# Four tiles ahead of the first projection: the odd 64 columns transposed twice by TensorE instead of normalised twice

## The chip, the cores and the metric

The kernel runs on one core of one Trainium2 chip. The metric is the time of one execution in device microseconds (us). Three runs of the kernel before took 221.12, 221.18 and 221.22 us; 221.18 is their median. Engine names as in the profile: PE is TensorE (PEld its weight loads), DVE is VectorE, ACT is ScalarE, POOL is GpSimd, SP is SyncE.

## What is computed

Attention within a sliding window of 256 and a gated feed-forward network run in parallel on one layer-normed input, and both are added to it (S = 2048 rows, D = 448 columns, 16 heads of 28, F = 1792):

```python
xn = _layernorm(x)                       # per row: (x - mean) / sqrt(var + 1e-5)
qkv = xn @ wqkv                          # q, k, v, 16 heads of 28
mask = (i - j >= 0) & (i - j < 256)
o = softmax(where(mask, q @ k.T * 28 ** -0.5, -1e9)) @ v
ffn = (gelu(xn @ w_gate) * (xn @ w_up)) @ w_down
out = x + o @ wo + ffn
```

## The kernel before

The 2048 rows are 16 tiles of 128 rows, and 4 blocks of 4 tiles. Nearly every product needs xn with its columns on the partitions, so each tile is normalised into `xn` (128 rows x 512 columns) and then transposed into `xnT`, four slices of 128 columns. 448 columns are three slices of 128 and one of 64. The odd 64 are kept twice: `norm` (L205) writes columns 0 to 447 with one instruction and columns 384 to 447 once more behind them, at 448 to 511, so that slice 3 holds the same 64 columns on partitions 0 to 63 and on 64 to 127. Products over the odd 64 then run in pairs, one in each half of PE's rows (`mm_half`, L231), and the weights' odd rows lie in the two halves likewise (`w3p`, `wraw[:, 3]`, `wv[:, 3]`).

Tiles 0 to 3 take the way through PE: `stat(t)` (L193: bn_stats and bn_aggr on DVE), `rstd(t, 1)` (L198: Ln and Exp on ACT), `norm(t)` (L208: the 448 columns on DVE, the 64 on Pool for tiles 1, 2, 5, 6, 7 and on DVE for the others), `transp` (L217: four PE transposes into one PSUM tile, then one copy into `xnT`, on ACT for tiles 0 to 2 and on DVE for tile 3). Later tiles are transposed by DMA (`dma_transp`, L213).

The order on each engine is the order of the program (the pool's scheduler is switched off by `manual_schedule`, L91), and it is written out by hand in L675 to L721. Ahead of it stand, in the order of the code: the loads of x and the weights on SP's and ACT's queues (L126 to L138), the identity and the fixed columns of `v_sb` on Pool (L141 to L143), and on DVE the memsets of `eps_t`, of `wo` (which also serves as data of the warm-up matmuls) and of the pads of `wqp`, `wkp` and `w3p` (L166 to L177). `warmup(n)` (L187) issues n matmuls of 128 x 512 on `wo` whose results nobody reads. Then, from L675:

- 8 warm-ups, tile 0 up to its transposes, statistics of tile 2, `norm(1)`, one more warm-up, tile 1's transposes, statistics of tile 3;
- `v_dense(0)` (L247: three matmuls over the full slices for the v of one tile), `norm(2)`, `pads` (L661: a group of heads of `wraw` copied into `wqp`'s padded layout) on DVE, the copy of `wraw[:, 3]` into `w3p` on DVE (L693), `pads` of `wkp` on ACT, tile 2's transposes, `v_dense(1)`, `norm(3)`;
- `make_masks` (L154) on Pool: a memset of `masks` to 1 and 18 affine_selects of 64 x 64; the first reader is `apply_masks` in block 1. Pool's own masking of block 0 (`masked`, L521) comes behind it on Pool;
- tile 3's transposes, `v_dense(2)`, then the first projections `s` (`proj`, L270, of `wqp` and `wkp` over the columns of all four tiles) and their odd 64 rows (`qk_halves`), q and k copies, `pads` of the second group of heads for `wqp` and `wkp`, copies of v, `v_dense(3)`, `pads` of the last two groups.

From there attention of block 0 runs with the projections and parts of the feed-forward network between its steps (L753 on).

Of the kernel before, what the change touches and what calls it, by code (L numbers as in the profile page):

```python
# [11 lines left out]
bf16 = mybir.dt.bfloat16  # L12
# [3 lines left out]
S, D, H, Dh, F = 2048, 448, 16, 28, 1792  # L16
P = 128
NT = S // P
NF = F // P
QB, NB = 512, 4  # L20
# [55 lines left out]
def kernel(  # L76
# [11 lines left out]
    nc = tc.nc  # L88
# [6 lines left out]
    psum = fast.enter_context(tc.tile_pool(name="psum", bufs=2, space=bass.MemoryType.PSUM))  # L95
# [18 lines left out]
    wraw = blk.tile([P, 4, 2 * D], bf16, name="wraw", tag="hT")  # L114
# [5 lines left out]
    wo = const.tile([P, 4, D], bf16, name="wo")  # L120
# [19 lines left out]
    ident = const.tile([P, P], bf16, name="ident")  # L140
# [11 lines left out]
    masks = const.tile([P, 3, 4, 64], bf16, name="masks")  # L152

    def make_masks():  # L154
        nc.gpsimd.memset(masks[:, :, :, :], 1.0)
        for i, edges in enumerate(EDGES):
            for j, (_, *kinds) in enumerate(edges):
                for h, kind in enumerate(kinds):
                    if kind:
                        m = masks[64 * h:64 * h + 64, i, j, :]  # L160
                        nc.gpsimd.affine_select(out=m, in_=m, pattern=[[kind, 64]], compare_op=ALU.is_ge, fill=0.0,
                                                base=min(kind, 0), channel_multiplier=-kind)
# [1 line left out]

    eps_t = const.tile([P, 1], f32, name="eps_t")
    nc.vector.memset(eps_t[:, :], 1e-5)  # L166
    nc.vector.memset(wo[:, :, :], 0.0)
    warm = wo[:, :, :].rearrange("p g n -> p (g n)")
    wqp = const.tile([P, 3, H, 32], bf16, name="wqp")
    wkp = const.tile([P, 3, H, 32], bf16, name="wkp")  # L170
    w3p = const.tile([P, H, 32], bf16, name="w3p")
# [3 lines left out]
    nc.vector.memset(wqp[:, :, :, Dh:32], 0.0)  # L175
    nc.vector.memset(wkp[:, :, :, Dh:32], 0.0)
    nc.vector.memset(w3p[:, :, Dh:32], 0.0)  # L177
    nc.scalar.preload_act_table_set("natural_log_exp_and_others")

    xnT = const.tile([P, 4, S], bf16, name="xnT")  # L180
# [6 lines left out]
    def warmup(n):  # L187
        wps = phase[0].pool.tile([P, 2, QB], f32, name="wps", tag="s")
        for i in range(n):
            nc.tensor.matmul(wps[:, i % 2, :], lhsT=warm[:, 0:P], rhs=warm[:, 0:QB], start=True, stop=True)  # L190


    def stat(t):  # L193
        st = work.tile([P, nc.vector.BN_STATS_DIM], f32, name="st")
        nc.vector.bn_stats(out=st[:, :], in_=x_sb[:, t, :])
        nc.vector.bn_aggr(out=mv_all[:, t, :], in_=st[:, :])
# [6 lines left out]
    xns = {}  # L203

    def norm(t):  # L205
        xn = work.tile([P, 4, P], bf16, name="xn", bufs=4)
        xf = xn[:, :, :].rearrange("p a b -> p (a b)")
        for eng, lo, n, src in ((nc.vector, 0, D, 0), (nc.gpsimd if t in (1, 2, 5, 6, 7) else nc.vector, D, 64, 384)):  # L208
            eng.tensor_scalar(out=xf[:, lo:lo + n], in0=x_sb[:, t, src:src + n], scalar1=mv_all[:, t, 0:1],
                              scalar2=rstd_all[:, t:t + 1], op0=ALU.subtract, op1=ALU.mult)  # L210
        xns[t] = xn
# [2 lines left out]

        nc.sync.dma_start_transpose(out=xnT[:, :, t * P:(t + 1) * P], in_=xns.pop(t)[:, :, :].rearrange("p a b -> p (a b)"))

    def transp(t, n, copy, tag):  # L217

        tp = psum.tile([P, 2, 4, P], bf16, name="tp", tag=tag, bufs=2 if tag == "m" else 1)
        for i in range(n):  # L220
            xn = xns.pop(t + i)
            for c in range(4):
                nc.tensor.transpose(out=tp[:, i, c, :], in_=xn[:, c, :], identity=ident[:, :])
        copy(out=xnT[:, :, t * P:(t + n) * P].rearrange("p c (i q) -> p i c q", q=P), in_=tp[:, 0:n, :, :])

    def mm3(ps, lhs, rhs, start, stop):
        for c in range(3):
# [12 lines left out]
    def bank(name):  # L240

        tag = ring[0][ring[1] % len(ring[0])]
        ring[1] += 1
        return psum.tile([P, QB], f32, name=name, tag=tag, bufs=2 if tag == "m" else 1)


    def v_dense(t, pv):  # L247
        mm3(pv, lambda c: xnT[:, c, t * P:(t + 1) * P], lambda c: wv[:, c, :], True, False)
# [4 lines left out]
    def v_copy(t, pv, copy):  # L253
        copy(out=v_sb[:, t, :, 0:Dh], in_=pv.rearrange("p (h d) -> p h d", d=Dh))
# [24 lines left out]
    def qk_copies(qb, g, pq, pk):  # L279
        ts = slice(qb * QB, (qb + 1) * QB)  # L280
        nc.scalar.copy(out=qT[:, g, ts], in_=pq)
        nc.vector.tensor_copy(out=kT[:, g, ts], in_=pk)
        done.add((qb, g))
# [377 lines left out]
    def pads(eng, dst, gs):  # L661

        hs = slice(4 * gs.start, 4 * gs.stop)
        c0 = D * (dst is wkp)
        src = wraw[:, 0:3, c0 + Dh * hs.start:c0 + Dh * hs.stop]
        eng(out=dst[:, :, hs, 0:Dh], in_=src.rearrange("p c (h d) -> p c h d", d=Dh))
# [5 lines left out]
    def alone(name, tag):  # L672
        return psum.tile([P, QB], f32, name=name, tag=tag, bufs=1)[:, 0:D]

    warmup(8)  # L675
    stat(0)
    rstd(0, 1)
    stat(1)
    rstd(1, 1)
    norm(0)  # L680
    transp(0, 1, nc.scalar.copy, "o")
    stat(2)
    norm(1)
    rstd(2, 1)
    warmup(1)
    transp(1, 1, nc.scalar.copy, "d")
    stat(3)
    rstd(3, 1)
    pvs = [bank("pv")[:, 0:D]]
    v_dense(0, pvs[0])  # L690
    norm(2)
    pads(nc.vector.tensor_copy, wqp, slice(0, 1))
    nc.vector.tensor_copy(out=w3p[:, :, 0:Dh], in_=wraw[:, 3, 0:D].rearrange("p (h d) -> p h d", d=Dh))  # L693
    pads(nc.scalar.copy, wkp, slice(0, 1))
    transp(2, 1, nc.scalar.copy, "o")
    pvs.append(bank("pv")[:, 0:D])
    v_dense(1, pvs[1])
    norm(3)
    make_masks()
    transp(3, 1, nc.vector.tensor_copy, "d")  # L700
    pvs.append(alone("pv", "o"))
    v_dense(2, pvs[2])
    pq, pk = (phase[0].pool.tile([P, 2, QB], f32, name="s0", tag="s")[:, 0, :] for _ in range(2))
# [6 lines left out]
    for t in range(2):  # L710
        v_half(t, pvs[t])
    qk_copies(0, 0, pq, pk)
    for dst in (wqp, wkp):
        pads(nc.vector.tensor_copy, dst, slice(1, 2))
    v_copy(0, pvs[0], nc.scalar.copy)
    v_copy(1, pvs[1], nc.vector.tensor_copy)
    pvs.append(alone("pv", "d"))
    v_dense(3, pvs[3])
    ring[1] = 0
# [114 lines left out]
    with tc.If(n_ok < 1, preferred_fallthrough_block=True, label="general"):  # L834
        general_path(tc, locals_=dict(x_sb=x_sb, xnT=xnT, qT=qT, kT=kT, v_sb=v_sb, wg=wg, wu=wu, wgu3=wgu3, wd=wd, wo=wo,
                                      ident=ident, outv=outv))
# [109 lines left out]
```

## Time and profile before

| | us |
|---|---|
| median of three runs (lowest, highest) | 221.18 (221.12, 221.22) |
| the profiled execution | 221.11 |
| its span in the trace | 219.4 |
| PE busy | 213.0 |
| DVE busy | 152.3 |
| ACT busy | 133.3 |
| POOL busy | 48.8 |

The profile shows one execution. A row of its timeline is the start, the length, the engine, the line of the kernel, the operation, output<-input with shapes, the count of instructions merged into the row, and in brackets how long the engine was idle before and for whom it waited. A matmul's length holds its way through the array, so several in a row overlap, and the distance between starts is the rate. The chain of waits goes back from the last instruction, at each step to what released it.

### The profile page before, as it was taken

How to read it: one execution, taken by the hardware profiler on the slowest of the kernel's cores; microseconds unless marked ns; L12 is line 12 of the kernel's file. 1: busy time of each engine (PE TensorE's matmuls, PEld its weight loads, DVE VectorE, ACT ScalarE, POOL GpSimd, SP SyncE). 2: the span in 40 equal slices, each digit the busy share in tenths (PEclk: the TensorE clock that was granted, in tenths of full speed). 3: DMA queues.
4: the chain of work that ended last, by engine and by line, in shares of the span. 5: the costliest groups of instructions: out<-in, count | busy, mean ns of one | idle time of the engine just before them, and what ended most of it. 6: DMA issues, size and time to landing. Idle time of an engine off the chain costs nothing.

```text
span 219.4 us, 5439 instructions
## 1 busy us (share of the span) xinstructions
PE 213.0 (97%) x2281; PEld 95.6 (44%) x2281; DVE 152.3 (69%) x345; ACT 133.3 (61%) x131; POOL 48.8 (22%) x83
## 2 busy tenths in 40 slices
PE   6999999999999999999999999999999999999993
PEld 2433333444444454444444445444344445444562
DVE  5987896799666883679565795386356799479521
ACT  3588788662878875432878888233486777565000
POOL 5767987320000120022000022021000022022001
PEclk9999999999999999999999999999999999999999
DMA  6994799203100001102400000200000000000001
GB/s 191 300 302 80 180 318 308 51 1 75 45 0 24 24 24 27 20 1 44 75 1 24 23 1 24 52 14 0 0 3 21 25 3 24 24 1 0 22 28 44
DMA packets 18045, 13.30 MB, mean 61 GB/s; under 512 B 8704, under 2 KB 16992, under 8 KB 18016
## 3 DMA queue, kind: packets, MB, share of 16 engines
q1 hardware_dynamic: 17072, 12.62, 21.5%
q8 instruction: 19, 0.31, 0.6%
q10 hardware_dynamic: 944, 0.29, 0.5%
q14 instruction: 10, 0.08, 0.1%
HBM read 9.15 MB, written 2.18 MB: 52 GB/s over the span
## 4 chain that ended last, share of the span: by engine, by line
PE 93%; DVE 3%; DMA 1%; ACT 1%; issue 1%; DVEq 0%
PE po L376 20%; PE gt L228 16%; PE u L228 12%; PE sc L612 6%; PE po L371 6%; PE gt L234 5%; PE ue L228 5%; PE ov L572 5%; PE pq L228 4%; PE pv L228 4%; PE pk L228 3%; PE pq L234 1%; PE g L228 1%; DMA x_sb<-in_A_x_dram 1%; PE ue L234 1%; PE pv L234 1%
## 5 line engine op out<-in xcount | busy, mean ns | idle before, releaser
L618 ACT ACTIVATE p_sb<-sc 128x2048 bf16<-128x2048 f32 (+2 forms) x42 | 73.8, 1758 | 12.6 <-PE sc L612 8.2
L376 PE MATMUL po<-wd,hT 128*128 128x448 bf16 (+1 forms) x238 | 49.8, 342 | 0.0
L460 ACT ACTIVATE ge<-gt 128x1024 bf16<-128x1024 f32 x26 | 26.6, 1024 | 34.9 <-PE u L234 20.1
L538 POOL TENSOR_TENSOR oN<-oc,l 128x512 bf16<-128x512 f32 x12 | 16.0, 1332 | 137.8 <-DVE l L552 87.4
L228 PE MATMUL gt<-xnT,wg 128*128 128x512 bf16 x156 | 37.5, 380 | 0.0
L467 DVE TENSOR_TENSOR hT<-ge,u 128x512 bf16<-128x512 bf16 x40 | 25.7, 682 | 12.9 <-ACT ge L460 12.9
L376 PEld LDWEIGHTS <-hT 128*128 128x128 bf16 x238 | 21.5, 98 | 18.8 <-issue 2.6
L228 PE MATMUL u<-xnT,wu 128*128 128x512 bf16 x120 | 29.2, 379 | 0.0
L519 DVE TENSOR_TENSOR p_sb<-p_sb,masks 128x256 bf16<-128x256 bf16 (+1 forms) x90 | 26.8, 352 | 0.4 <-ACT p_sb L618 0.4
L228 PEld LDWEIGHTS <-wg 128*128 128x128 bf16 x168 | 15.3, 98 | 21.3 <-issue 4.5
L228 PEld LDWEIGHTS <-wu 128*128 128x128 bf16 x168 | 16.0, 98 | 19.2 <-issue 1.0
L557 DVE TENSOR_TENSOR oc<-oc,ov 128x512 f32<-128x512 f32 x12 | 8.2, 687 | 16.5 <-ACT oc L556 16.5
L612 PE MATMUL sc<-qT,kT 28*64 28x320 bf16 (+7 forms) x640 | 16.9, 263 | 0.2
L411 DVE CAST hT<-ue 128x512 bf16<-128x512 f32 x16 | 10.2, 682 | 8.3 <-PE ue L234 8.3
L371 PE MATMUL po<-wo,oN 128*128 128x448 bf16 (+1 forms) x68 | 15.9, 342 | 0.0
L381 DVE TENSOR_TENSOR res<-po,x_sb 128x448 bf16<-128x448 f32 (+1 forms) x17 | 10.0, 586 | 8.6 <-PE po L376 8.4
L529 POOL TENSOR_SCALAR_AFFINE_SELECT p_sb<-p_sb 128x512 bf16<-128x512 bf16 (+1 forms) x20 | 14.2, 730 | 5.5 <-ACT p_sb L618 5.4
L234 PE MATMUL gt<-xnT,wgu 64*128 64x512 bf16 (+1 forms) x67 | 12.7, 380 | 0.0
L556 ACT COPY oc<-ov 128x512 f32<-128x512 f32 x12 | 7.0, 584 | 8.7 <-PE ov L572 8.7
L228 PE MATMUL pq<-xnT,wqp 128*128 128x512 bf16 x45 | 12.2, 380 | 0.0
L544 DVE STREAM_TRANSPOSE l<-oc 128x512 f32<-128x512 f32 x16 | 11.3, 704 | 1.4 <-POOL oN L538 1.2
L228 PE MATMUL ue<-xnT,wu 128*128 128x512 bf16 x48 | 12.0, 380 | 0.0
(94 smaller groups left out, 242.7 us busy)
## 6 DMA issues: line engine op xcount, KB each, us to landing
out_dram<-res SPq DMA_DIRECT2D x15, 112.0 KB
x_sb<-in_A_x_dram SPq DMA_DIRECT2D x3, 448.0 KB
wu<-in_B_w_up_dram SPq DMA_DIRECT2D x1, 1344.0 KB
wg<-in_B_w_gate_dram SPq DMA_DIRECT2D x1, 1344.0 KB
wd<-in_B_w_down_dram SPq DMA_DIRECT2D x3, 448.0 KB
wraw<-in_A_wqkv_dram SPq DMA_DIRECT2D x2, 252.0 KB
wo<-in_A_wo_dram SPq DMA_DIRECT2D x4, 98.0 KB
wv<-in_A_wqkv_dram SPq DMA_DIRECT2D x1, 336.0 KB
```

What stands on the lines that cost most here:

```text
L228: nc.tensor.matmul(ps, lhsT=lhs(c), rhs=rhs(c), start=start and c == 0, stop=stop and c == 2, skip_group_check=True)
L234: nc.tensor.matmul(ps[c:c + m], lhsT=lhs[p0:p0 + 64, c:c + m], rhs=rhs[p0:p0 + 64], start=start, stop=stop, tile_position=(p0, c), skip_gr ...
L371: nc.tensor.matmul(po[:, 0:w], lhsT=oN[:, g, cs], rhs=wo[:, g, lo:up], start=(g == 0), stop=False, skip_group_check=True)
L376: nc.tensor.matmul(po[:, 0:w], lhsT=hT[:, f, cs], rhs=wd[:, f, lo:up], start=False, stop=(f == NF - 1), skip_group_check=True)
L460: nc.scalar.activation(out=ge[:, :, :], in_=pr["gt"][:, :, :], func=ACT.Gelu_apprx_tanh)
L467: nc.vector.tensor_tensor(out=hT[:, f + i, :], in0=ge[:, i, :], in1=u, op=ALU.mult)
L519: nc.vector.tensor_tensor(out=reg, in0=reg, in1=m, op=ALU.mult)
L529: nc.gpsimd.affine_select(out=reg, in_=reg, pattern=mid + [[1 if diag else -1, min(w, P)]], compare_op=ALU.is_ge, fill=0.0, base=0 if diag ...
L538: nc.gpsimd.tensor_tensor(out=oN[:, g, :], in0=oc[:, :], in1=inv, op=ALU.mult)
L544: nc.vector.transpose(out=l1[:, :, :].rearrange("p a b -> p (a b)"), in_=oc[:, :])
L612: nc.tensor.matmul(ss[k0:k0 + nk, j, col:col + nq], lhsT=kT[r, g, kt * P + k0:kt * P + k0 + nk], rhs=qT[r, g, qb * QB + q0:qb * QB + q0 + ...
L618: nc.scalar.activation(out=p_sb[:, :, 0:ncol], in_=ss[:, :, 0:ncol], func=ACT.Exp, scale=SCALE)
```

## The change

`norm` of tiles 0 to 3 writes only the 448 columns. `transp` issues three transposes of 128 columns and two of the last 64, the one into partitions 0 to 63 and the other into 64 to 127 of the same PSUM slice (`tile_position` 0 and 64). The memset of `masks` moves from Pool to DVE, behind the pads' memsets and ahead of tile 0. A memset of one column of `masks` on DVE behind `norm(3)` and the `w3p` copy makes Pool's affine_selects wait for that point. The memset of `wo` is split into its first 512 columns, which the warm-ups read, and the rest; ten warm-ups stand where there were eight. The `w3p` copy moves behind `norm(3)`, `pads` of `wkp` on ACT behind tile 2's copy, and `pads` of `wkp`'s second group on DVE behind the copy of v of tile 1.

```diff
     def make_masks():
-        nc.gpsimd.memset(masks[:, :, :, :], 1.0)
         for i, edges in enumerate(EDGES):
...
-    nc.vector.memset(wo[:, :, :], 0.0)
     warm = wo[:, :, :].rearrange("p g n -> p (g n)")
+    for c in (slice(0, QB), slice(QB, 4 * D)):
+        nc.vector.memset(warm[:, c], 0.0)
...
     nc.vector.memset(w3p[:, :, Dh:32], 0.0)
+    nc.vector.memset(masks[:, :, :, :], 1.0)
...
-        for eng, lo, n, src in ((nc.vector, 0, D, 0), (nc.gpsimd if t in (1, 2, 5, 6, 7) else nc.vector, D, 64, 384)):
+        both = ((nc.vector, 0, D, 0), (nc.gpsimd if t in (5, 6, 7) else nc.vector, D, 64, 384))
+        for eng, lo, n, src in both if t > 3 else both[:1]:
...
-    def transp(t, n, copy, tag):
-
-        tp = psum.tile([P, 2, 4, P], bf16, name="tp", tag=tag, bufs=2 if tag == "m" else 1)
-        for i in range(n):
-            xn = xns.pop(t + i)
-            for c in range(4):
-                nc.tensor.transpose(out=tp[:, i, c, :], in_=xn[:, c, :], identity=ident[:, :])
-        copy(out=xnT[:, :, t * P:(t + n) * P].rearrange("p c (i q) -> p i c q", q=P), in_=tp[:, 0:n, :, :])
+    def transp(t, copy, tag):
+
+
+        tp = psum.tile([P, 8, P], bf16, name="tp", tag=tag, bufs=1)
+        xn = xns.pop(t)
+        for c in range(3):
+            nc.tensor.transpose(out=tp[:, c, :], in_=xn[:, c, :], identity=ident[:, :])
+        for p0 in (0, 64):
+            nc.tensor.transpose(out=tp[p0:p0 + 64, 3, :], in_=xn[:, 3, 0:64], identity=ident[:, :], tile_position=(0, p0))
+        copy(out=xnT[:, :, t * P:(t + 1) * P], in_=tp[:, 0:4, :])
...
-    warmup(8)
+    warmup(10)
...
     pads(nc.vector.tensor_copy, wqp, slice(0, 1))
-    nc.vector.tensor_copy(out=w3p[:, :, 0:Dh], in_=wraw[:, 3, 0:D].rearrange("p (h d) -> p h d", d=Dh))
-    pads(nc.scalar.copy, wkp, slice(0, 1))
-    transp(2, 1, nc.scalar.copy, "o")
+    transp(2, nc.scalar.copy, "o")
     pvs.append(bank("pv")[:, 0:D])
     v_dense(1, pvs[1])
     norm(3)
+    pads(nc.scalar.copy, wkp, slice(0, 1))
+    nc.vector.tensor_copy(out=w3p[:, :, 0:Dh], in_=wraw[:, 3, 0:D].rearrange("p (h d) -> p h d", d=Dh))
+    nc.vector.memset(masks[:, 0, 0, 0:1], 1.0)
     make_masks()
-    transp(3, 1, nc.vector.tensor_copy, "d")
+    transp(3, nc.vector.tensor_copy, "d")
...
-    for dst in (wqp, wkp):
-        pads(nc.vector.tensor_copy, dst, slice(1, 2))
+    pads(nc.vector.tensor_copy, wqp, slice(1, 2))
     v_copy(0, pvs[0], nc.scalar.copy)
     v_copy(1, pvs[1], nc.vector.tensor_copy)
+    pads(nc.vector.tensor_copy, wkp, slice(1, 2))
```

More of the change, by code (lines that the diff above doesn't have):

```diff
@@ L680 @@
     norm(0)
-    transp(0, 1, nc.scalar.copy, "o")
+    transp(0, nc.scalar.copy, "o")
     stat(2)
@@ L685 @@
     warmup(1)
-    transp(1, 1, nc.scalar.copy, "d")
+    transp(1, nc.scalar.copy, "d")
     stat(3)
```

## The prediction

> **What bounds the kernel now.** First the page: its first lines, then its chain of work that ended last.
>
> ```profile
> span 219.4 us, 5439 instructions
> PE 213.0 (97%) x2281; PEld 95.6 (44%) x2281; DVE 152.3 (69%) x345; ACT 133.3 (61%) x131; POOL 48.8 (22%) x83
> PE 93%; DVE 3%; DMA 1%; ACT 1%; issue 1%; DVEq 0%
> ```
>
> TensorE (PE) holds the chain for 93% of the span. The other 7% is worth having if it lies ahead of all PE work. So the second view is the chain over the first 30 us (start, length, what), and its beginning is the only place that the diff touches.
>
> ```profile
> 0.80 2.65 DMA x_sb<-in_A_x_dram
> ...
> 7.82 0.87 DVE w3p L693
> 8.69 0.32 DVE xn L209
> ...
> 9.06 0.44 PE tp L223 x4
> ```
>
> The chain waits for tile 0 of x, runs on VectorE (DVE) until tile 3 is normalised at 9.01, and goes on with PE's transposes of it at 9.06; PE keeps it from there for nearly all of the span. What the change is worth is therefore the move of one instant: the first projection `s<-xnT,wqp`, which needs all four transposed tiles. The third view, the timeline of the first 16 us (start, length, engine), gives the prices. I write "start to start" for the distance between two rows, since neighbours overlap by 0.05 to 0.1 us.
>
> ```profile
> 1.18 0.81 DVE L167 MEMSET wo<- 128x896 uint32 x1 [0.16 <-issue]
> 2.04 3.60 PE L190 MATMUL wps<-wo 128*128 128x512 bf16 x8 [2.04 <-DVE wo L167]
> 2.11 1.53 POOL L143 MEMSET v_sb<- 128x768 bf16 x1
> 2.16 0.09 DVE L177 MEMSET w3p<- 128x32 uint32 x1
> 3.47 0.63 DVE L195 BATCH_NORM_STATS2 st<-x_sb 128x6 f32<-128x448 bf16 x1 [1.23 <-DMA x_sb<-in_A_x_dram]
> 4.68 0.20 ACT L201 ACTIVATE rstd_all<-lnv 128x1 f32<-128x1 f32 x1
> 4.96 0.36 DVE L209 TENSOR_SCALAR xn<-x_sb,mv_all,rstd_all 128x448 bf16<-128x448 bf16 x1
> 5.24 0.29 DVE L209 TENSOR_SCALAR xn<-x_sb,mv_all,rstd_all 128x64 bf16<-128x64 bf16 x1
> 5.43 0.63 PE L223 MATMUL tp<-ident,xn 128*128 128x128 bf16 x4
> 5.45 0.62 DVE L195 BATCH_NORM_STATS2 st<-x_sb 128x6 f32<-128x448 bf16 x1
> 5.86 0.63 PE L190 MATMUL wps<-wo 128*128 128x512 bf16 x1
> 6.10 0.58 ACT L224 COPY xnT<-tp 128x512 bf16<-128x512 bf16 x1 [0.49 <-PE tp L223]
> 6.20 0.37 DVE L209 TENSOR_SCALAR xn<-x_sb,mv_all,rstd_all 128x448 bf16<-128x448 bf16 x1
> 6.58 0.30 ACT L200 ACTIVATE lnv<-mv_all,eps_t 128x1 f32<-128x1 f32 x1
> 6.62 0.49 PE L223 MATMUL tp<-ident,xn 128*128 128x128 bf16 x4
> 6.91 0.20 ACT L201 ACTIVATE rstd_all<-lnv 128x1 f32<-128x1 f32 x1
> 6.95 0.73 PE L228 MATMUL pv<-wv,xnT 128*128 128x448 bf16 x3
> 7.15 0.58 ACT L224 COPY xnT<-tp 128x512 bf16<-128x512 bf16 x1
> 7.52 0.30 DVE L666 COPY wqp<-wraw 128x336 bf16<-128x336 bf16 x1
> 7.63 0.30 ACT L200 ACTIVATE lnv<-mv_all,eps_t 128x1 f32<-128x1 f32 x1
> 7.74 0.95 DVE L693 COPY w3p<-wraw 128x448 bf16<-128x448 bf16 x1
> 7.83 0.73 POOL L155 MEMSET masks<- 128x768 bf16 x1
> 7.96 0.20 ACT L201 ACTIVATE rstd_all<-lnv 128x1 f32<-128x1 f32 x1
> 8.07 0.45 ACT L666 COPY wkp<-wraw 128x336 bf16<-128x336 bf16 x1
> 8.61 0.39 DVE L209 TENSOR_SCALAR xn<-x_sb,mv_all,rstd_all 128x448 bf16<-128x448 bf16 x1
> 10.01 0.81 PE L228 MATMUL s<-xnT,wqp 128*128 128x512 bf16 x3
> ```
>
> The last row is that projection, at 10.01.
>
> **The change part by part.**
>
> *DVE's line to tile 3.* Gone are the 64-column normalisation of tile 0 (5.24 to 5.45 start to start: 0.21), `w3p` ahead of tile 3 (7.74 to 8.61: 0.87), and tile 3's own 64 columns, on which its fourth transpose waited. DVE alone could start tile 3's normalisation (xn3) near 8.61 - 0.21 - 0.87 = 7.53. What is late next is the factor that xn3 needs: ScalarE (ACT) makes it in program order behind the copies of the transposed tiles 0 and 1. That line starts with ACT's copy of tile 0, which waits for PE; I call its start T0 (6.10 now).
>
> *ACT's line from T0 to xn3.* Copy to Ln 0.48 (6.10 to 6.58), Ln to Exp 0.33 (6.58 to 6.91), Exp to the next copy 0.11 (7.96 to 8.07), copy to Ln 0.48 (7.15 to 7.63), Ln to Exp 0.33 (7.63 to 7.96), Exp to a normalisation on DVE 0.28 (4.68 to 4.96): 2.01 together. xn3 starts at T0 + 2.01.
>
> *PE ahead of T0.* The first memset shrinks from 896 to 256 words. Between 32 words at 0.09 and 896 at 0.81 that is 0.28, so PE starts 0.53 earlier, at 1.51. The eight warm-ups took 2.04 to 5.43, 0.424 each; ten end at 1.51 + 4.24 = 5.75. Tile 0's columns could be used 0.42 after their normalisation starts (6.20 to 6.62 for tile 1), at 5.38, so at this clock the two extra warm-ups hold the transposes up by 0.32. The four transposes ran 5.43 to T0 = 6.10, which is 0.67, with 0.107 from one to the next. The fourth becomes two of 64 columns side by side, and PE has to change to another tile shape first. That change has rows:
>
> ```profile
> 10.66 0.81 PE L228 MATMUL s<-xnT,wkp 128*128 128x512 bf16 x3
> 11.40 0.39 PE L234 MATMUL s<-xnT,w3p 64*128 64x512 bf16 x2
> ```
>
> Three 512-column matmuls from 10.01 take 0.65, so those from 10.66 are issued by 11.31, and the 64-row pair starts at 11.40: 0.09 for the change of shape. The two of that pair start together. At half the clock I take 0.12; 0.23 if the two 64-column transposes run one behind the other. T0 = 5.75 + 0.67 + 0.12 = 6.54 (6.65 at the worse bound). xn3 starts at 8.55, against 8.61.
>
> *From xn3 to the projection.* Transposes 0.45 later (8.61 to 9.06). Then the copy of tile 3:
>
> ```profile
> 9.06 0.44 PE L223 MATMUL tp<-ident,xn 128*128 128x128 bf16 x4 [0.32 <-DVE xn L209]
> 9.53 0.42 DVE L224 COPY xnT<-tp 128x512 bf16<-128x512 bf16 x1 [0.33 <-PE tp L223]
> ```
>
> It came 0.47 after the first transpose. With the change of shape but no wait for late columns I take 0.53 (bounds 0.47 and 0.47 + 0.09). Copy to projection 0.48. So 8.55 + 0.45 + 0.53 + 0.48 = 10.01: **no move at all**.
>
> *`w3p` now runs between xn3 and that copy.* It starts 0.28 after xn3 (4.96 to 5.24), at 8.83, under the transposes, which give it until 9.53. Its 0.95 of now lies over Pool's memset of the masks, 7.83 to 8.56, and it ends 0.13 after that memset; 336 elements of the same kind of copy took 0.30 at 7.52. Without Pool beside it I take 0.35, ending at 9.18, then a memset of one column; hidden. Were the 0.87 its own, it would end at 9.70 and cost 0.17: the upper bound. The Trainium skill (SBUF — State Buffer, Who interferes with whom) says that VectorE copies in a two-port mode and any GpSimd instruction exclude each other for a whole instruction. By that rule the sum has 0.35, without it 0.87; the trace agrees with the rule here, in that one row.
>
> *The masks.* DVE's memset of 768 elements, at 0.83 ns each as between the two memsets above, is about 0.7. It starts near 2.3 and ends near 3.0; the wait for x to 3.47 hides it, with 0.5 to spare. Pool's 18 mask operations start near 9.25 instead of 8.63:
>
> ```profile
> 8.63 4.92 POOL L161 TENSOR_SCALAR_AFFINE_SELECT masks<-masks 64x64 bf16<-64x64 bf16 x18
> 15.11 1.70 POOL L529 TENSOR_SCALAR_AFFINE_SELECT p_sb<-p_sb 128x1024 bf16<-128x1024 bf16 x2 [1.56 <-ACT p_sb L618]
> ```
>
> With 4.92 they end near 14.2, and Pool's next work waits for ACT until 15.11: 0.9 to spare. Pool no longer normalises 64 columns of tiles 1 and 2; only PE's fourth transposes waited for those.
>
> *`wkp` behind the copy of v.* Swapped on DVE, the second `wkp` piece would be ready about where that copy ended; PE's use follows within 0.1. I take 0, with 0 to +0.1 as bounds. `wkp`'s first piece on ACT goes behind the third copy and is needed only 0.65 into the projections: 0. No DMA is added or moved, SP's queue is unchanged, and the four tiles after the first are not touched.
>
> *Sum.* 0.00 us at the projection, bounds -0.06 to +0.4 (upwards 0.11 for the pair, 0.03 for the copy, 0.17 for `w3p`, 0.1 for `wkp`). The profiled execution took 221.11 beside a span of 219.4; the runs shown have a median of 221.18, 0.07 more. Forecast 221.1.
>
> **The rivals.**
>
> *The clock rises earlier.* All of the above has PE at half speed until T0. In the trace a warm-up still takes 0.63 at 5.86, while three 448-column matmuls take 0.73 together from 6.95: the rise is between 5.9 and 6.95, at most 4.9 after the first matmul. The same delay counted from 1.51 gives at most 6.4, too late to help, hence my forecast. But nothing shows that the delay is a constant. If the rise comes by about 5.2, the ten warm-ups end in time, the transposes start at 5.38 and T0 is 5.38 + 0.53 = 5.91. Then tile 1 binds: xn1 at 6.20 - 0.21 = 5.99, its transposes 0.42 later (6.20 to 6.62), its copy 0.53 later, 6.94; plus 0.48 + 0.33 + 0.28 xn3 is at 8.03, the copy of tile 3 at 9.01, the projection at 9.49. That is -0.52, **220.6**. Between the two, each 0.1 of T0 is worth 0.1. For it: the warm-ups start earlier and leave no gap. Against it: the one rise that the trace shows. The Trainium skill (TensorE: Matmul & The Clock Gate, Part 1: The HAM clock gate) speaks of free-running windows of 3.4 us and a rise around 4 us into sustained work; counted from 1.51 that would be 5.5, T0 about 6.2, and some 220.8. No run here shows that figure.
>
> *The clock rises later still: slower.* The place is PE between tiles 1 and 3. At half speed a 448-column triple takes 3 x 0.37 = 1.11, and 0.57 at full (6.95 + 0.73 less a tail of 0.16). The transposes of tiles 0 and 1 with two changes of shape each take 0.43 + 2 x 0.12 = 0.67, the warm-up between them 0.42, so the first triple runs from 5.75 + 2 x 0.67 + 0.42 = 7.51 to 8.62. With the rise at R in that stretch it ends at (8.62 + R) / 2; tile 2's transposes at 0.42 and the second triple at 0.57 follow, and tile 3's should start at 9.00. That holds up to R = 7.4; at 8.6 they start at 9.60, 0.6 late: **221.7**. Against it: before's one rise lies below 7.
>
> *Pool blocks DVE's masks memset.* If it had to wait for Pool's memset of v (2.11 to 3.64) it would end at 4.35 and start tile 0's statistics 0.88 late; of that, 0.5 survives behind the warm-ups (tile 0's transposes at 5.38 + 0.88 = 6.26 against 5.75): **221.6**. Against it: the short memset at 2.16 took its 0.09 beside that very memset.
>
> **How the numbers follow.** Clock as in the trace, no move: 0.43. Rise during the last warm-up or tile 0's transposes, -0.1 to -0.44: 0.15. Early rise, beyond -0.44: 0.33. Late rise: 0.05. Memset blocked: 0.04. A measurement of this kernel tells 0.2%, 0.44 us, from no change. So faster 0.33, same 0.43 + 0.15 = 0.58, slower 0.09. The range goes from the early rise with 0.1 beneath it for shifts behind the projection, 220.5, to the forecast with most of its upper bounds, 221.4.
>
> **What would show it.** The start of the projection `s<-xnT,wqp` (10.01 now) against the time. PE's first warm-up near 1.5. T0 at 6.54: if it is near 5.9, the clock was early, and the warm-ups' lengths show it. xn3 2.0 behind T0: if it follows DVE instead, my line through ACT is wrong. `w3p` at about 0.35. The forecast is wrong if PE's clock rises at another instant than in this one execution, which is the term I know least.

## The result, and the profile after

| | before | after |
|---|---|---|
| median, us | 221.25 | 220.66 |
| lowest to highest | 220.92 to 221.92 | 220.26 to 221.15 |
| executions | 22 | 22 |
| ratio, 95% interval | | 0.997, 0.9964 to 0.9977 |
| the profiled execution | 221.11 | 221.15 |

The change made the kernel 0.59 us, 0.3%, faster. That is inside the range on record (220.5 to 221.4), but it is the time of a rival (the clock rises earlier, 220.6, chance 0.33) and not of the forecast (221.1). The profiled execution of the changed kernel is the slowest of its 22, and it follows the forecast. The instant at which PE's clock rises, which differs from one execution to the next, accounts for most of the difference between the two, as far as the runs below show. When x lands, and what follows the last matmul, differ as well.

The first lines of the page after, then its chain of waits (share of the span by engine):

```profile
span 219.4 us, 5447 instructions
PE 213.9 (98%) x2287; PEld 96.1 (44%) x2287; DVE 152.1 (69%) x346; ACT 133.3 (61%) x131; POOL 46.9 (21%) x80
PE 96%; ACT 1%; DVE 1%; issue 1%; DVEq 0%
```

PE's share of the chain went from 93% to 96%, DVE's from 3% to 1%. The chain of waits over the first 30 us of the kernel after (start, length, engine, what):

```profile
1.05 0.28 DVE wo L168
1.38 4.45 PE wps L191 x10
5.82 0.32 PE tp L225 x3
...
6.39 0.58 ACT xnT L228
...
7.44 0.41 DVE xn L211
```

Before, this stretch began with the load of x and ran along DVE. In this execution it begins with the memset for the warm-ups: PE's own cold work holds up tile 0, and not the data. The timeline of the kernel after gives the answers to the terms of the sum (start, length, engine, line, operation, output<-input):

```profile
1.38 4.45 PE L191 MATMUL wps<-wo 128*128 128x512 bf16 x10 [1.38 <-DVE wo L168]
2.12 1.53 POOL L143 MEMSET v_sb<- 128x768 bf16 x1
2.36 0.70 DVE L178 MEMSET masks<- 128x768 bf16 x1
3.51 0.63 DVE L196 BATCH_NORM_STATS2 st<-x_sb 128x6 f32<-128x448 bf16 x1 [0.45 <-DMA x_sb<-in_A_x_dram]
5.61 0.53 PE L225 MATMUL tp<-ident,xn 128*128 128x128 bf16 x3
6.07 0.27 PE L227 MATMUL tp<-ident,xn 128*64 128x128 bf16 x2
6.28 0.39 PE L191 MATMUL wps<-wo 128*128 128x512 bf16 x1
6.39 0.58 ACT L228 COPY xnT<-tp 128x512 bf16<-128x512 bf16 x1 [0.74 <-PE tp L227]
8.34 0.40 DVE L211 TENSOR_SCALAR xn<-x_sb,mv_all,rstd_all 128x448 bf16<-128x448 bf16 x1 [0.32 <-ACT rstd_all L202]
8.34 0.74 PE L232 MATMUL pv<-wv,xnT 128*128 128x448 bf16 x3
8.65 0.27 DVE L702 COPY w3p<-wraw 128x448 bf16<-128x448 bf16 x1
8.92 0.33 PE L225 MATMUL tp<-ident,xn 128*128 128x128 bf16 x3
9.00 4.99 POOL L160 TENSOR_SCALAR_AFFINE_SELECT masks<-masks 64x64 bf16<-64x64 bf16 x18 [5.35 <-DVE masks L703]
9.47 0.42 DVE L228 COPY xnT<-tp 128x512 bf16<-128x512 bf16 x1 [0.54 <-PE tp L227]
9.95 0.81 PE L232 MATMUL s<-xnT,wqp 128*128 128x512 bf16 x3
```

The lengths of the matmuls tell the clock. Ten warm-ups at 0.42 each, against 0.21 for a matmul of the same size from 9.95 on, lie at half speed, and so do tile 0's transposes at 5.61; the warm-up at 6.28 takes 0.39, which is full speed. So the clock rose between 6.07 and 6.28; the trace's own events of the granted clock put it at 6.17 (6.85 before). The ten warm-ups thus held tile 0's transposes back to 5.61, as forecast (with eight of them and x landing at the same instant, the transposes started at 5.42), and the projection came at 9.95 instead of 10.01.

The kernel "64 columns twice again" below has the same warm-ups and, but for the odd 64 columns, the same order, and its profiled execution (220.56) fell to the other side. Its timeline:

```profile
1.38 3.61 PE L191 MATMUL wps<-wo 128*128 128x512 bf16 x10 [1.38 <-DVE wo L168]
3.35 0.63 DVE L196 BATCH_NORM_STATS2 st<-x_sb 128x6 f32<-128x448 bf16 x1 [0.30 <-DMA x_sb<-in_A_x_dram]
5.26 0.44 PE L225 MATMUL tp<-ident,xn 128*128 128x128 bf16 x4 [0.27 <-DVE xn L211]
5.74 0.58 ACT L226 COPY xnT<-tp 128x512 bf16<-128x512 bf16 x1 [0.25 <-PE tp L225]
7.98 0.61 DVE L211 TENSOR_SCALAR xn<-x_sb,mv_all,rstd_all 128x448 bf16<-128x448 bf16 x2 [0.32 <-ACT rstd_all L202]
9.39 0.81 PE L230 MATMUL s<-xnT,wqp 128*128 128x512 bf16 x3
```

Here ten warm-ups took 3.61 in place of 4.45: the clock rose at 4.01, the transposes waited for DVE and not for PE, and the projection came at 9.39. The rival had said 9.49. Not all of the 0.56 between 9.95 and 9.39 is the clock's: x landed earlier too (statistics of tile 0 at 3.35 against 3.51), and where tile 0 waits for DVE, these 0.16 count.

### The profile page after: what moved, and what is told of

It reads as the page before. It is cut to its first block, busy times and chain, and to the rows that moved or that the text cites. A ratio compares the mean times of both kernels' runs of the same rounds, so it can differ in the third digit from the quotient of the medians.

```text
span 219.4 us, 5447 instructions
## 1 busy us (share of the span) xinstructions
PE 213.9 (98%) x2287; PEld 96.1 (44%) x2287; DVE 152.1 (69%) x346; ACT 133.3 (61%) x131; POOL 46.9 (21%) x80
## 4 chain that ended last, share of the span: by engine, by line
PE 96%; ACT 1%; DVE 1%; issue 1%; DVEq 0%
PE po L380 20%; PE gt L232 16%; PE u L232 12%; PE sc L616 6%; PE po L375 6%; PE gt L238 5%; PE ue L232 5%; PE ov L576 5%; PE pq L232 4%; PE pv L232 4%; PE pk L232 3%; PE wps L191 2%; PE pq L238 1%; PE g L232 1%; PE ue L238 1%; PE pv L238 1%
```

## The experiments

The theories, with the letters that the expectations use. **A**: both halves are needed, a shorter line to tile 3 and a PE that starts early and warms up without a gap, since the line counts only where the clock is up in time. **B**: the warm-ups are all of the gain. **C**: the line is all of it. **D**: the number of warm-ups sets the clock, and gaps between them don't matter. **E**: the doubled transposes are the core. In the first four expectations A is only the line through ACT with Pool's memset holding DVE; the clock came into it after those four runs. The kernels ran in three groups; each ratio is to the kernel before as run beside it (medians 221.35, 221.54 and 221.69 in the three groups).

**w3p alone.** The kernel before with one line moved.

```diff
-    nc.vector.tensor_copy(out=w3p[:, :, 0:Dh], in_=wraw[:, 3, 0:D].rearrange("p (h d) -> p h d", d=Dh))
...
     norm(3)
+    nc.vector.tensor_copy(out=w3p[:, :, 0:Dh], in_=wraw[:, 3, 0:D].rearrange("p (h d) -> p h d", d=Dh))
     make_masks()
```

> The kernel before with one edit: the w3p copy stands behind tile 3's normalisation. Theory A (the chain runs through ACT's line from the copy of tile 0, and VectorE is held up by Pool's masks memset through a shared port): the memset, 7.83 to 8.56 in the trace of before, now holds up tile 3's normalisation itself, so the projection moves by -0.1 to +0.1 us and the time stays at 221.2. Theory C (the 0.87 of w3p on the chain is the gain): -0.4 us or more, 220.8 or less. Theory B (the earlier and longer warm-ups are the gain): no change.

Measured: 221.24 (12 executions, 220.59 to 221.72), ratio 0.9997 (0.9983 to 1.0011). The time is as expected. In the profiled execution the projection moved more than expected, to 9.71. Timeline of that kernel, first Pool, then DVE and PE:

```profile
7.83 0.73 POOL L155 MEMSET masks<- 128x768 bf16 x1
8.17 0.52 DVE L209 TENSOR_SCALAR xn<-x_sb,mv_all,rstd_all 128x448 bf16<-128x448 bf16 x1 [0.34 <-ACT rstd_all L201]
8.82 0.27 DVE L698 COPY w3p<-wraw 128x448 bf16<-128x448 bf16 x1
9.71 0.81 PE L228 MATMUL s<-xnT,wqp 128*128 128x512 bf16 x3
```

With `w3p` out of the way, tile 3's normalisation runs into Pool's memset instead: it takes 0.52 in place of 0.39 and ends at 8.69, 0.13 after the memset's 8.56. That is what happened to `w3p` before (8.69 and 8.56 as well), and `w3p` itself now takes 0.27. The clock rose at 6.78 and x landed at 3.47, nearly as in the profile of before (6.85 and 3.47), so the 0.30 at the projection is the line's. The time, 221.09 against 221.11, doesn't show it: what follows the last matmul took 3.82 here and 3.63 before, and the time outside the trace 0.11 more.

**w3p and masks.** The same, and the masks' memset on DVE ahead of tile 0, with the selects held back.

```diff
-        nc.gpsimd.memset(masks[:, :, :, :], 1.0)
...
+    nc.vector.memset(masks[:, :, :, :], 1.0)     # behind the pads' memsets
...
+    nc.vector.memset(masks[:, 0, 0, 0:1], 1.0)   # behind w3p
     make_masks()
```

> The kernel before with two edits: w3p behind tile 3's normalisation, and the masks' memset on VectorE ahead of tile 0 with Pool's selects held back. Theory A: nothing of Pool's beside tile 3 but ACT's line binds; tile 3's normalisation at about 8.2 instead of 8.61, its odd 64 columns and w3p behind it, -0.3 us (-0.2 to -0.45), 220.9. Theory C: the same as the w3p edit alone, -0.4 or more in both. Theory B: no change.

Measured: 221.41 (12, 220.66 to 222.73), ratio 1.0008 (0.9993 to 1.0023). The expectation missed. Its one profiled execution (220.66, the fastest of the 12) shows the gain that the median doesn't. The timeline of PE in it:

```profile
2.04 3.59 PE L190 MATMUL wps<-wo 128*128 128x512 bf16 x8 [2.04 <-DVE wo L166]
5.78 0.38 PE L190 MATMUL wps<-wo 128*128 128x512 bf16 x1
9.51 0.81 PE L228 MATMUL s<-xnT,wqp 128*128 128x512 bf16 x3
```

The warm-up behind tile 0 took 0.38, against 0.63 before: the clock rose at 5.68, and the projection came 0.50 earlier. The other executions of the same kernel ended up to 2.1 us later. So these two edits shorten the line, and most executions don't show it.

**The changed kernel with the old warm-ups.** One memset of `wo`, eight warm-ups.

```diff
-    for c in (slice(0, QB), slice(QB, 4 * D)):
-        nc.vector.memset(warm[:, c], 0.0)
+    nc.vector.memset(wo[:, :, :], 0.0)
...
-    warmup(10)
+    warmup(8)
```

> The changed kernel with the warm-ups of before: one memset of wo, 8 warm-ups. They end at 5.43 at the slow clock as in before, where tile 0 is ready. Theory A: ACT's copy of tile 0 at about 6.2 with the clock still slow, tile 3's normalisation at about 8.2, projection 9.5 to 9.8: -0.3 to -0.6 against before, as fast as the changed kernel within 0.2 us. Theory B: the gain is gone, 221.2.

Measured: 220.96 (12, 220.58 to 221.54), ratio 0.9984 (0.9973 to 0.9995): -0.39 of medians, as expected. By the ratios it is 0.3 short of the changed kernel, where at most 0.2 was expected; the intervals overlap. The projection of its profiled execution is at 10.19, behind the 9.5 to 9.8 expected, with a rise as late as 7.93. Theory B doesn't give the -0.39.

**The changed kernel with eight warm-ups and the early start.** The split memset stays.

```diff
-    warmup(10)
+    warmup(8)
```

> The changed kernel with 8 warm-ups instead of 10, memset still split: they end at about 4.8 at the slow clock, ahead of tile 0. Theory A: tile 0's transposes never wait for warm-ups, start at 5.4; ACT's copy of tile 0 at 5.9 to 6.2; time 220.5, at or up to 0.2 below the changed kernel, with less spread, unless the gap on PE lets the clock rise later. Theory B: fewer warm-ups lose part of the gain, 220.8 to 221.0.

Measured: 220.87 (12 executions), ratio 0.9996 (0.9974 to 1.0018). Less spread was expected, and there is more: eight executions of 220.18 to 221.17 and four of 222.07 to 222.59. The profiled one (221.17) is of the lower group. Its timeline of PE:

```profile
1.37 3.60 PE L191 MATMUL wps<-wo 128*128 128x512 bf16 x8 [1.37 <-DVE wo L168]
5.42 0.50 PE L225 MATMUL tp<-ident,xn 128*128 128x128 bf16 x3 [0.45 <-DVE xn L211]
6.10 0.39 PE L191 MATMUL wps<-wo 128*128 128x512 bf16 x1
```

Two warm-ups fewer than in the changed kernel leave a hole of 0.45 on PE ahead of tile 0. With it, a third of the executions lost 0.9 to 1.4 us more than the worst of the others. That a whole step of the clock slipped in them is argued, since none of those four was profiled. It would not be all: the profiles without warm-ups below, with the clock rising at 9.03 and 9.21, have the projection at 10.36 and 10.59, which with the shorter endings of the other profiles is an estimated 221.3 to 222.0.

**Warm-ups alone.** The kernel before with the split memset and ten warm-ups.

```diff
-    nc.vector.memset(wo[:, :, :], 0.0)
+    for c in (slice(0, QB), slice(QB, 4 * D)):
+        nc.vector.memset(warm[:, c], 0.0)
...
-    warmup(8)
+    warmup(10)
```

> The kernel before with the warm-up edits alone: memset of wo split, ten warm-ups. Theory A, as the first four runs have it: the PE clock rises at another instant in each execution, one counted window after PE's start, so a start 0.66 us earlier moves the rise in all of them; the shorter line to tile 3 counts only where the rise is early. Here VectorE's line stays, tile 3's normalisation at 8.5 to 8.6, projection not before 9.9; early executions stay at 221.1, late ones become rarer: median -0.1 to -0.25 against before. Theory B (the earlier warm-ups are the whole gain): -0.5 to -0.6.

Measured: 221.36 (12, 220.59 to 221.58), ratio 0.9996 (0.9983 to 1.001): 0.18 below the median beside it, not clear of nothing. Theory B, which asked for 0.5 to 0.6, falls. The timeline of Pool and DVE shows what an early clock (5.04 in this execution) meets in the old order:

```profile
7.45 0.85 POOL L155 MEMSET masks<- 128x768 bf16 x1
7.49 0.89 DVE L667 COPY wqp<-wraw 128x336 bf16<-128x336 bf16 x1
7.67 0.82 DVE L694 COPY w3p<-wraw 128x448 bf16<-128x448 bf16 x1
8.41 0.59 DVE L210 TENSOR_SCALAR xn<-x_sb,mv_all,rstd_all 128x448 bf16<-128x448 bf16 x2
```

`w3p` still stands in front of tile 3. Pool's memset now holds up the copy into `wqp` ahead of it (0.89 in place of 0.30), and `w3p` ends at 8.49, 0.19 behind that memset's 8.30. The projection was at 9.81, against 9.51 and 9.39 in the executions above with rises at 5.68 and 4.01 that have `w3p` behind.

**Nine and twelve warm-ups**, all else as in the changed kernel.

```diff
-    warmup(10)
+    warmup(9)      # in the other kernel: warmup(12)
```

> The changed kernel with nine warm-ups: they end at 5.2 at the slow clock, 0.2 us ahead of tile 0's transposes, where eight left 0.65 and ten leave none. Theory A (a gap on PE makes a window not count, and the rise slips by a whole window): 8 warm-ups had 4 of 12 executions above 222; with 9 at most 1 or 2 of 12, the others at 220.3 to 220.8, median 220.5 to 220.7. Theory D (the clock counts warm-ups, not gaps): about as many slow executions as half of those with eight, and median between 8 and 10 warm-ups.

Measured: 220.61 (7, 220.24 to 220.81), ratio 0.9955 (0.9938 to 0.9973). No late group, as theory A asked, and a median below both eight's and ten's, where D asked for one between. With seven executions neither is beyond doubt.

> The changed kernel with twelve warm-ups: at the slow clock they end near 6.45 and hold up tile 0's transposes. Theory A: nothing changes where the rise comes by about 5, up to 0.8 us more where it comes late: lowest about 220.3, median 220.8 to 221.1, highest 221.6 or more. Theory D (more warm-ups, earlier clock): median at or below that of ten, 220.6 or less.

Measured: 221.42 (12), ratio 0.9989 (0.9972 to 1.0005): four executions of 220.44 to 220.74 and eight of 221.21 to 221.81. The lowest and the highest are as expected, the median is worse, since more executions than expected paid. D, which asked for a median at or below that of ten, falls here. The timeline of PE in a paying one (221.80):

```profile
1.38 5.30 PE L191 MATMUL wps<-wo 128*128 128x512 bf16 x12 [1.38 <-DVE wo L168]
6.47 0.45 PE L225 MATMUL tp<-ident,xn 128*128 128x128 bf16 x3
```

The clock rose at 6.72, so all twelve ran cold, tile 0 began at 6.47 where the changed kernel's began at 5.61 (2 x 0.43 later), and the projection came at 10.70 instead of 9.95.

**The 64 columns twice again.** The changed kernel with the 64 columns normalised twice and four full transposes, everything else kept.

```diff
-        for eng, lo, n, src in both if t > 3 else both[:1]:
+        for eng, lo, n, src in both:        # Pool for tiles 1 and 2 again
...
-        for c in range(3):
+        for c in range(4):
...
-        for p0 in (0, 64):
-            nc.tensor.transpose(out=tp[p0:p0 + 64, 3, :], in_=xn[:, 3, 0:64], identity=ident[:, :], tile_position=(0, p0))
```

> The changed kernel with the odd 64 columns normalised twice again (Pool for tiles 1 and 2, VectorE for 0 and 3) and four full transposes. Theory A: 0.2 us more on VectorE behind tile 0, 0.3 behind tile 3, and PE's fourth transposes wait for Pool in tiles 1 and 2; against that no change of tile shape on PE, 0.1 each: projection later by 0 to 0.3 at an equal rise of the clock, median 220.7 to 220.9. Rival E (the doubled transposes are the core of the gain): 0.4 or more lost, 221.1.

Measured: 220.74 (12, 220.5 to 221.19), ratio 0.9972 (0.996 to 0.9984), against 0.997 for the whole change. Theory E falls: with the new warm-ups, the edit that names the change is worth nothing that shows.

**The changed kernel and the nine warm-ups once more**, side by side.

> The changed kernel itself, beside the next three on one chip. Theory A: 220.3 to 221.1, median 220.6 to 220.7; its profile gives one more pair of the clock's rise and the projection's start: T0 is 0.78 behind the first transpose, and the projection at 9.4 if the rise is before 5, up to 10.0 if it is at 6.2 or later.

> The changed kernel with nine warm-ups, once more, now beside the one with ten. Theory A: up to 0.3 us less per execution where the rise is late, the same where it is early, and now and then one that slips by a window: median 0 to 0.15 below ten. Theory D (number of warm-ups sets the clock): above ten by 0.1 or more.

Measured: ten 220.93 (11, 220.25 to 221.17), ratio 0.9961 (0.9947 to 0.9975); nine 220.69 (7, 220.41 to 220.94), ratio 0.9956 (0.9941 to 0.9972). The ten, expected at 220.6 to 220.7, fall into five executions up to 220.50 and six from 220.93, and the median lies at the foot of the upper group. The profiled one is again of the upper group; its timeline of PE:

```profile
5.62 0.53 PE L225 MATMUL tp<-ident,xn 128*128 128x128 bf16 x3
6.32 0.61 PE L191 MATMUL wps<-wo 128*128 128x512 bf16 x1
10.00 0.81 PE L232 MATMUL s<-xnT,wqp 128*128 128x512 bf16 x3
```

The warm-up at 6.32 is still cold (rise at 7.21), and the projection is at 10.00, the forecast's 10.01. Nine gives 0.24 less beside ten, where 0 to 0.15 was expected. The two intervals overlap, so nine is not shown to be better; it has the lowest median in both groups, and none of its 14 executions is above 221.

**No warm-ups**, in the kernel before and in the changed one.

```diff
-    warmup(8)      # in the other kernel: warmup(10)
```

> The kernel before without its 8 warm-ups ahead of tile 0 (the one between tiles 0 and 1 stays). PE's first work is at 5.4. The ten profiles so far have the rise 2.6 to 5.9 us behind PE's first matmul; so now at 8.0 to 11.3, behind all that the tiles need. Theory A: 222.0 to 223.3, median 222.6, PE's slow triples bind. Theory B' (the start of the line on VectorE binds all the same): 221.5.

> The changed kernel without its ten warm-ups ahead of tile 0. With the rise at 8.0 to 11.3 PE binds in both kernels, and the changed one has the change of tile shape in addition, about 0.12 twice a tile at the slow clock, less one wait: Theory A: the gain is gone, 0 to +0.5 against the kernel before without warm-ups, 222.6 to 223.1. Theory C (the shorter line to tile 3 is worth its 0.5 by itself): -0.4 to -0.6 against it.

Measured: 222.86 (6, 222.52 to 223.45), ratio 1.0061 (1.0041 to 1.0082), and 222.90 (10, 222.18 to 224.07), ratio 1.0063 (1.0042 to 1.0083). Both medians lie where theory A expected them, and B', 221.5, falls. Without warm-ups the changed kernel is no faster than the one before: theory C, which asked for 0.4 to 0.6, falls, and A (0 to 0.5) holds at its lower end; in the two profiles the projection is 0.23 later with the change. The timeline of PE in the changed kernel without warm-ups:

```profile
7.18 1.30 PE L232 MATMUL pv<-wv,xnT 128*128 128x448 bf16 x3
8.28 0.53 PE L225 MATMUL tp<-ident,xn 128*128 128x128 bf16 x3
8.98 0.74 PE L232 MATMUL pv<-wv,xnT 128*128 128x448 bf16 x3
```

The triple at 7.18 takes 1.30 cold, the one at 8.98 takes 0.74. Cold PE work now stands between tiles 1 and 3, and the shorter line on DVE and ACT ends ahead of it. It doesn't account for the whole loss: the projections lie 0.35 and 0.58 behind that of before, the times of the same two executions 1.52 and 1.07. The rest comes behind the last matmul, and no run shows whether it has to do with the warm-ups.

All profiled executions together, in order of the projection's start. "x" is the start of tile 0's statistics, which wait for x. "Rise" is the instant in the trace's events from which the full clock was granted. "Tail" is what follows the last matmul in the trace.

| kernel | first matmul | x | rise | T0 | xn3 | projection | tail | time |
|---|---|---|---|---|---|---|---|---|
| 64 twice again | 1.38 | 3.35 | 4.01 | 5.74 | 7.98 | 9.39 | 3.70 | 220.56 |
| w3p and masks | 2.04 | 3.43 | 5.68 | 5.98 | 8.06 | 9.51 | 3.70 | 220.66 |
| nine again | 1.38 | 3.36 | 6.46 | 6.06 | 8.01 | 9.62 | 3.63 | 220.72 |
| w3p alone | 2.04 | 3.47 | 6.78 | 6.09 | 8.17 | 9.71 | 3.82 | 221.09 |
| nine | 1.38 | 3.48 | 6.09 | 6.19 | 8.14 | 9.74 | 3.54 | 220.75 |
| changed, eight | 1.37 | 3.51 | 6.08 | 6.21 | 8.16 | 9.77 | 3.81 | 221.17 |
| warm-ups alone | 1.37 | 3.44 | 5.04 | 5.83 | 8.41 | 9.81 | 3.47 | 220.75 |
| changed | 1.38 | 3.51 | 6.17 | 6.39 | 8.34 | 9.95 | 3.74 | 221.15 |
| changed again | 1.37 | 3.41 | 7.21 | 6.43 | 8.51 | 10.00 | 3.59 | 221.17 |
| before | 2.04 | 3.47 | 6.85 | 6.10 | 8.61 | 10.01 | 3.63 | 221.11 |
| changed, old warm-ups | 2.04 | 3.48 | 7.93 | 6.24 | 8.40 | 10.19 | 3.49 | 221.14 |
| before, none | 5.38 | 3.46 | 9.21 | 6.02 | 8.49 | 10.36 | 4.81 | 222.63 |
| changed, none | 5.40 | 3.48 | 9.03 | 6.19 | 8.34 | 10.59 | 4.12 | 222.18 |
| twelve | 1.38 | 3.57 | 6.72 | 7.14 | 9.09 | 10.70 | 3.64 | 221.80 |

From the projection's start to the end of the last matmul all 14 take the same, 205.74 to 205.75, so these edits act on PE's work through the projection alone. The tail differs by up to 0.35 even among the kernels with warm-ups, so one pair of times says little about a few tenths: "nine" and "changed, eight" are 0.03 apart at the projection and 0.42 in time. With eight and nine warm-ups the projection comes 6.26 behind x in all three executions, though the clock rises between 6.08 and 6.46: there x sets the instant, and not the clock.

## Why the prediction was right, and where it was wrong

**The step that failed** is the one under "The clock rises earlier": "The same delay counted from 1.51 gives at most 6.4, too late to help, hence my forecast." One execution's rise was taken as the kernel's. The table shows in its place that the delay from the first matmul to the rise differs from one execution to the next: 2.63 (64 twice again) to 5.89 (changed, old warm-ups), and 4.79 and 5.83 in two executions of the changed kernel itself. The traces of before (4.81) and of after (4.79) both lie within this spread. The chances of 0.43 for the late clock and 0.33 for the early one should have been nearer the other way round, by the recorded clocks below. The range held because it took in the rival as well as the forecast.

**What was right of it.** Given a late clock, the sum was right: T0 6.39 (forecast 6.54, 0.13 of it from PE's earlier start at 1.38), xn3 1.95 behind T0 (2.01), the projection at 9.95 (10.01), the time 221.15 (221.1). Given an early clock, the rival's sum came close too: 9.39 in place of 9.49, 220.56 in place of 220.6, though in a kernel that normalises the 64 columns twice, and with x 0.12 earlier than in the profile on which the sum was built. That the changed kernel's median (220.66) lies on that side because most of its executions have an early clock is an inference, since its own two profiled executions are both late ones.

**What the recorded clocks add.** Each execution has its mean granted clock on record. In the traces it reads 1.00 ahead of the rise too, so it falls short of 1.000 only where the clock falls before the end; and the fall comes 211.63 behind the rise in every such trace (last section). So where it is short, the rise is an estimate: the span, less twice the shortfall times the span, less 211.63. In the eight profiled executions where this can be done it is within 0.2 of the events. Of the changed kernel's 33 executions in two groups, 12 are short, with estimated rises of 6.0 to 7.2, and took 220.84 to 221.17; the 21 at 1.000 took 220.25 to 220.84. A reading of 1.000 goes with rises of 4.01 and 5.04, but also with some of 6.72 and later, so this supports the inference without proving it. With `w3p` alone, the times follow the estimated rise: 220.59 and 220.65 at 5.9, 221.01 to 221.53 from 6.3 to 6.9, 221.59 to 221.72 from 7.3 on. The kernel before, in the same group, hardly does: 221.13 to 221.38 up to 6.3, 221.13 to 222.01 from 7.3 on. That is what a shorter line gives if it counts only where the clock rises in time.

**Where the 0.59 comes from.** Of the ratio, the line without the 64-column edit and the `wkp` moves and with the old warm-ups gives nothing (1.0008), the warm-ups on the old line give 0.0004, the whole line with the old warm-ups 0.0016, all of it 0.003, and the changed kernel without any warm-ups nothing against its like. So neither half alone carries all of it: the line brings about half with the old warm-ups, and nothing without any. The intervals, some 0.001 either way, allow no finer split. A mechanism that agrees with these: the shorter line brings the projection forward where the clock rises in time for PE's work ahead of tile 3 (`w3p` alone, rise at 6.78: 0.30 earlier), and not where it rises later (changed with the old warm-ups, 7.93: at 10.19); PE's start 0.66 earlier (2.04 to 1.38) puts more executions on the first side. That warm-ups without a hole keep them there is argued from the kernel with eight.

**Sizes.** xn3 to tile 3's transposes took 0.58 (8.34 to 8.92) and not 0.45: the three matmuls of `v_dense(1)` at 8.34 stand in front on PE. The change of tile shape cost 0.14 at half clock, where I took 0.12: the first 64-column transpose came 0.24 behind the third full one in the kernel after (5.83 to 6.07 in the trace), where full ones follow each other at 0.107. `w3p` took 0.27 (0.35), and the masks' memset 0.70 (0.7), 2.36 to 3.06, with 0.45 of waiting for x behind it (0.5). Pool's selects ended at 13.99, ahead of Pool's next work at 15.05.

**The other rivals.** Pool blocking the masks' memset fell: that memset ran from 2.36 beside Pool's own memset (2.12 to 3.65) and took the 0.70 forecast. The late clock as a loss (221.7) did not come in the changed kernel's 33 executions, none above 221.17. Whether the four executions above 222 with eight are of this kind is open.

**Open.** Why the line without the 64-column edit and the `wkp` moves gave 221.41 and with them 220.96 with the old warm-ups, while the 64-column edit is worth nothing that shows with the new ones. What sets the tail, and why it was longest without warm-ups. What happened in the four late executions with eight warm-ups. Whether nine is better than ten.

## What to carry to other kernels

The first microseconds of this kernel, where PE is cold, differ from one execution to the next; one profile shows one draw, so price such a change for an early and a late clock and take the median of many executions. Start warm-ups as early as their data allow and end them close to the first real work, not beyond it: with two fewer than ten, 4 of 12 executions were above 222, with two more the median was 221.42 in place of 220.66, and nine, which end 0.1 to 0.2 before tile 0, did at least as well as ten. A shorter line on another engine ahead of PE pays only where PE's own cold work isn't the later of the two. Compare single profiles by the instant that the change moves, and not by the whole time, when the end of the kernel varies as it does here.

## What the runs showed of the hardware

The lag from the first matmul to the full clock spread over 3.26 us (2.63 to 5.89) in 14 profiled executions. The fall of the clock behind the last work tells more. The windows of the last microseconds (columns: window, length, then share busy and count of PE, PEld, DVE, ACT and POOL, then the granted clock) of the kernel after, then of before:

```profile
217.00:218.00 1.00, 0.00 (x0) 0.00 (x0) 0.06 (x1) 0.00 (x0) 0.07 (x1) 0.90 0.21 56
218.00:219.00 1.00, 0.00 (x0) 0.00 (x0) 0.00 (x0) 0.00 (x0) 0.00 (x0) 0.50 0.02 8
```

```profile
217.00:218.00 1.00, 0.00 (x0) 0.00 (x0) 0.06 (x1) 0.00 (x0) 0.14 (x1) 1.00 0.21 57
218.00:219.00 1.00, 0.00 (x0) 0.00 (x0) 0.00 (x0) 0.00 (x0) 0.00 (x0) 0.74 0.02 8
```

Full clock for 0.80 of the microsecond from 217 makes 0.90, so the clock fell at 217.80 after, and for 0.48 of that from 218 at 218.48 before. Both are 211.63 behind the rise (6.17 and 6.85), though the work differs, and 211.63 is 62 x 3.4133. In three others (warm-ups alone, twelve, 64 twice again) the events give 215.04, 63 x 3.4133. So in all 14 executions rise and fall lie a whole number of steps of 3.41 apart, as on a grid. The Trainium skill (TensorE: Matmul & The Clock Gate, Part 1: The HAM clock gate) speaks of a free-running window of 3413 ns that doesn't start with the kernel; the trace agrees. It also says that the transition varies by 500 ns either way; the 3.26 measured here is nearly a whole window, and the measurement decides.

Pool's memset of the masks held whichever DVE instruction met it: `w3p` before, which ended 0.13 behind it, tile 3's normalisation with `w3p` alone, 0.13 behind, and with the warm-ups alone the copy into `wqp`, 0.08 behind, with `w3p` next at 0.19.
